# Attention with a feed-forward stage on one core: the products with v of the first eight heads in pieces, their sums in two banks of their own

## The chip, the core and the metric

One Trainium2 chip; the program runs on one of its cores. A core has TensorE (PE, matrix products; PEld is its weight load), VectorE (DVE), ScalarE (ACT), GpSimd (POOL) and SyncE (SP, which here only starts transfers). Each engine takes its instructions in the order in which they were written for it. Matrix products write to PSUM, which has eight banks of 512 fp32 values per partition; VectorE and ScalarE read them from there. The metric is the device time of one execution in microseconds. Time before: 1236.84 us, the median of 3 runs (1234.63 to 1239.13).

## The reference

For 8 batches and 8 heads with 576 positions and 64 values per head, attention with a block-causal mask (blocks of 64), then a feed-forward stage over all 4608 tokens:

```python
scores = scale * np.matmul(q, k.transpose(0, 1, 3, 2))
scores = np.where(mask, scores, -1000000000.0)
scores = scores - np.max(scores, axis=-1, keepdims=True)
attn = np.exp(scores)
attn = attn / (np.sum(attn, axis=-1, keepdims=True) + 1e-09)
out = np.matmul(attn, v)                # x: 4608 tokens x 512
h = x @ w_in                            # 512 -> 2048
sp = np.maximum(h, 0.0) + np.log1p(np.exp(-np.abs(h)))
g = h * erf(sp)
y = g @ w_out                           # 2048 -> 512
```

## The kernel before, in words

**Steps.** A loop `for n in range(N + 3)` (L684) runs over the 64 heads, software-pipelined. Step n holds: the load of head n+3 (L396 to L402: k and q into a ring of four tiles, by POOL's queue, and into a staging tile by SyncE's); the low parts of k and q on POOL (L405, L408), the latter for the first twelve heads behind two copies on ScalarE (L415); the scores of head n+2 for the row maxima (`maxes`: products L432, VectorE's reduction L435, five parts); the transposed maxima of head n+1 (L462, L464, a small transfer L465 into the ring); and the scores of head n once more, transposed, with the maxima taken off, and their exponentials (`probs`: products L478 and L479, ScalarE L483, six parts). In every even step from 2 on, `pv` (L502) takes the products of the probabilities of heads n-2 and n-1 with v. Four heads form a group `qd` of one load of v; NQ = 2 groups make a batch. In the step after a group's second pair, `normalise` (L579) transposes and inverts the row sums, scales the result and stores it to `x_d`, split into two fp16 parts.

**The rest of a step.** In the first twenty steps the weights are converted too (`conv`: load L115 on SyncE's queue, ScalarE L122 and L128, VectorE L123 to L125; then `split_w`, L148 and L149). The feed-forward stage (`moe1`: products L193 and L202, the function of `gate` between them) takes its turns in each step once the first batch has been stored, from step 10 on, and runs alone after the last head.

**Order.** Each part of a step is a list of small functions with a stretch of the step, from 0 to 1. `merged` (L210) gives entry i of a list of m the place lo + (hi - lo)(i + 0.5)/m and calls all of them by place. That order is the priority by which the framework's planner orders each engine's instructions; it works with modelled durations, and an instruction that is ready may be put before an earlier one that is not. Waits between engines are inserted by the framework.

**pv.** `go` (L518) handles one half of the 576 query positions (0 to 255, 256 to 575): for every key block of 128 up to the half's end it issues the products of both heads, 64 columns of the array each, summing into one bank `u`; after the last key block ScalarE copies the sum out (L530). The first half has two key blocks, the second five. `sums` (L544) adds the probabilities up with products of 32 columns of ones (L550) into one bank, which ScalarE reads (L552, L553). For the first three batches the operands are fp32, and each product is two passes of TensorE. `pv` returns two entries: all of `go` for both halves, and `sums`.

**Banks.** PSUM is split into three pools: `ps_a` (four banks), `ps_h` (two, the hidden values of the feed-forward stage) and `ps_o` (two, its outputs). `bank` (L321) hands out a bank for everything in attention. Until the first feed-forward job is loaded it goes round in eights: two requests of eight get a bank of `ps_h`, one of `ps_o`, five of `ps_a`. After that all come from `ps_a`. A request waits until the last reader of the bank's previous content is through.

Of the kernel before, what the change touches and what calls it, by code (L numbers as in the profile page):

```python
# [9 lines left out]
F32 = mybir.dt.float32  # L10
# [22 lines left out]
def tile_attention_moe(ctx: ExitStack, tc: tile.TileContext, qk, v, w, maskrows, selws, out):  # L33
# [5 lines left out]
    P = 128  # L39
    NCC = DM // P  # L40
    SCALE = 0.125
    NQ = H // 4
# [16 lines left out]
    ps_o = ctx.enter_context(tc.tile_pool(name="ps_o", bufs=2, space=PSUM))  # L59
# [70 lines left out]
    def scale_w(g, bank):  # L130

        rs = cpool.tile([P, 2], F32, name=f"wrs{g}")
        nc.vector.tensor_reduce(out=rs, in_=wss[g], axis=AX.X, op=ALU.add)
        pt = bank(f"wt{g}")
        nc.tensor.matmul(pt[:, :2], lhsT=ones, rhs=rs, start=True, stop=True)
        e = cpool.tile([P, 2], F32, name=f"we{g}")
        nc.vector.tensor_copy(e, pt[:, :2])
        nc.vector.tensor_scalar(out=i32(e), in0=i32(e), scalar1=23, scalar2=None, op0=ALU.logical_shift_right)
        nc.vector.tensor_scalar(out=i32(e), in0=i32(e), scalar1=131, scalar2=None, op0=ALU.add)
        nc.vector.tensor_scalar(out=i32(e), in0=i32(e), scalar1=1, scalar2=None, op0=ALU.logical_shift_right)  # L140
        powers(wsb[g][:, 0:2], wsb[g][:, 2:4], e, 15)
# [156 lines left out]
    with tc.tile_pool(name="apool", bufs=2) as apool, tc.tile_pool(name="spool", bufs=1) as spool, \  # L298
# [22 lines left out]
        def bank(name):  # L321

            turn.append(0)
            k = len(turn) % 8 if not loaded else 0
            if k in (2, 5):
                return ps_h.tile([P, 512], F32, tag="h", name=name)
            if k in (3,):
                return ps_o.tile([P, 512], F32, tag="o", name=name)
            return ps_a.tile([P, 512], F32, tag="a", name=name)

        def load_v(b, qd, src):
# [12 lines left out]
        def scale_v(b, qd, v32, vt):  # L344

            nm = f"{b}_{qd}"
            vm = apool.tile([P, 1], F32, tag="vm", name=f"vm{nm}")
            nc.vector.tensor_reduce(out=vm, in_=v32, axis=AX.XY, op=ALU.max, apply_absolute_value=True)
            pt = bank(f"vt{nm}")
            nc.tensor.transpose(out=pt[:1, :P], in_=vm, identity=ident)  # L350
            if qd == 0:
                nc.vector.tensor_reduce(out=top_v[b], in_=pt[:1, :P], axis=AX.X, op=ALU.max)
                if b < B32:
                    return
            vs = apool.tile([1, 2], F32, tag="vs", name=f"vs{nm}")
            vs_[b, qd] = vs
            e = apool.tile([1, 2], F32, tag="ve", name=f"ve{nm}")
            if qd:
                nc.vector.tensor_reduce(out=e[:, :1], in_=pt[:1, :P], axis=AX.X, op=ALU.max)
                nc.vector.tensor_tensor(out=e[:, :1], in0=e[:, :1], in1=top_v[b], op=ALU.max)  # L360
            nc.vector.tensor_scalar(out=i32(e[:, :1]), in0=i32(e[:, :1] if qd else top_v[b]), scalar1=23, scalar2=None, op0=ALU.logical_shift_right)
            nc.vector.tensor_scalar(out=i32(e[:, :1]), in0=i32(e[:, :1]), scalar1=77, scalar2=197, op0=ALU.max, op1=ALU.min)
            powers(vs[:, 0:1], vs[:, 1:2], e[:, :1], 10)
# [138 lines left out]
        def pv(qd, pp, prs, V, usb, rs):  # L502

            vv = V[1:]
            terms = ((0, 0), (1, 0), (0, 1)) if len(vv) > 1 else ((0, 0),)
            one, tail = (ones32, ones32t) if len(vv) > 1 else (ones[:, :32],) * 2
            st = {}

            def ranges(q0, q1):

                for j in range(5):
                    if starts[j] < q1:
                        a = max(q0, starts[j])
                        pt, c = offs[j]
                        c += a - starts[j]
                        yield j, min(P, S - j * P) if len(vv) == 1 else P, a - q0, pt, slice(c, c + q1 - a)

            def go(hf, j0, j1):  # L518
                q0, q1 = halves[hf]
                todo = list(ranges(q0, q1))  # L520
                if j0 == 0:
                    st[hf] = bank(f"u{qd}_{pp}_{hf}")
                u = st[hf]
                for j, kk, a, pt, cs in todo[j0:j1]:
                    for iv, ip in terms:
                        for hd in range(2):
                            nc.tensor.matmul(u[64 * hd : 64 * hd + 64, a : q1 - q0], lhsT=vv[iv][:kk, 2 * pp + hd, j, :], rhs=prs[hd][pt][ip][:kk, cs],  # L527
                                             start=j == 0 and (iv, ip) == terms[0], stop=j == todo[-1][0] and (iv, ip) == terms[-1])
                if j1 >= len(todo):
                    nc.scalar.copy(usb[:, q0:q1], u[:, : q1 - q0])  # L530


            order = []
            for hf, (q0, q1) in enumerate(((0, SH), (SH, S))):
                at, todo = 0, list(ranges(q0, q1))
                for n_, (j, kk, a, pt, cs) in enumerate(todo):
                    for k in range(len(vv)):
                        first, last = n_ == 0 and k == 0, n_ == len(todo) - 1 and k == len(vv) - 1
                        for hd in range(2):
                            order.append((at, hf, hd, k, j, kk, a, q1 - q0, pt, cs, first, last))  # L540
                        at += q1 - q0 - a
            order.sort(key=lambda o: o[0])

            def sums(n0, n1):  # L544
                if n0 == 0:
                    st["us"] = bank(f"us{qd}_{pp}")
                u = st["us"]
                for _, hf, hd, k, j, kk, a, w_, pt, cs, first, last in order[n0:n1]:
                    g = 2 * hf + hd
                    nc.tensor.matmul(u[32 * g : 32 * g + 32, a:w_], lhsT=(one if j < 4 else tail)[:kk, :], rhs=prs[hd][pt][k][:kk, cs], start=first, stop=last)  # L550
                if n1 >= len(order):
                    nc.scalar.activation(rs[:, : S - SH], u[:, : S - SH], AF.Identity, bias=eps)  # L552
                    nc.scalar.activation(rs[:64, S - SH :], u[:64, S - SH : SH], AF.Identity, bias=eps[:64])  # L553

            return [lambda: (go(0, 0, 2), go(1, 0, 5)), lambda: sums(0, len(order))]

        known = []
# [126 lines left out]
        for n in range(N + 3):  # L684
# [14 lines left out]
            qd = n // 4 + 1  # L699
# [8 lines left out]
            if n % 2 == 0 and 2 <= n <= N:  # L708
                j = n // 2 - 1
                qd, pp = divmod(j, 2)  # L710
                usbs[j] = apool.tile([P, S], F32, tag="usb", name=f"usb{j}", bufs=2)
                steps = pv(qd, pp, [prs.pop(2 * j), prs.pop(2 * j + 1)], vs[qd], usbs[j], rss[j % 2])
                lists.append((late("pv", steps), 0, 1))
                if pp == 1:
                    normals[n + 1] = qd
            if n in normals:
                qd = normals.pop(n)
# [67 lines left out]
```

## Time and profile before

| | |
|---|---|
| median of 3 runs | 1236.84 us (1234.63 to 1239.13) |
| the profiled execution | 1233.12 us, span 1231.3 us |
| mean granted clock of TensorE | 0.968 |
| TensorE busy | 1149.8 us (93%) |
| ScalarE busy | 863.3 us (70%) |
| VectorE busy | 824.7 us (67%) |
| POOL busy | 478.7 us (39%) |
| products with v, L527, in the first 180 us | 176 recorded passes |

The page gives shares over the whole span, which here mixes three stages: the first 100 us or so, where attention alone runs beside the conversion of the weights; the long middle, where attention and the feed-forward stage share the engines; and the end, where the feed-forward stage runs alone. In a row of a timeline stand the start, the duration, the engine, the line, what is written from what, the shapes and the count of merged instructions; in brackets the idle time before it and what ended it. A row of waits reads: who waited for whom, us in total, times, the longest. The granted clock is a share of full speed.

### The profile page before, as it was taken

Reading aid. Unit: us, or ns where it says so; the run is one execution under the profiler, and the core shown is the slowest. Engines: PE = TensorE matmul, PEld = TensorE weight load, DVE = VectorE, ACT = ScalarE, POOL = GpSimd, SP = SyncE. Lnnn points to the kernel's source line nnn. Section 1 sums busy time; section 2 is a strip of 40 time slices with the busy share of each in tenths; the row PEclk is TensorE's granted clock in tenths of the full one; section 3 lists DMA queues with packets and bytes.
Section 4 is the critical chain, followed back from the end, with each engine's and each line's share of the span. In section 5 each row is a group of like instructions: output and inputs, shape, how many; then the busy total and the mean of one; then the engine's idle time right before and its main releaser. Section 6 shows DMA issues by size and latency. Waiting matters only on the chain.

```text
span 1231.3 us, 23115 instructions
## 1 busy us (share of the span) xinstructions
PE 1149.8 (93%) x8874; PEld 796.0 (65%) x8874; DVE 824.7 (67%) x1559; ACT 863.3 (70%) x1675; POOL 478.7 (39%) x459
## 2 busy tenths in 40 slices
PE   6867899899999999999999999999989999999997
PEld 3545666566666667767666676776766766666663
DVE  5877887797577767677667666666667644455555
ACT  4665777577677776777777676777767776766664
POOL 7454545535444544445354444435444322100000
PEclk9876899989999999999999999999999999999999
DMA  8676667735545455453554455444544221221202
GB/s 231 171 211 161 166 186 219 179 91 122 120 133 138 110 129 124 129 136 102 124 137 95 114 125 121 115 124 116 120 114 108 57 67 57 72 69 52 65 23 85
DMA packets 94091, 148.19 MB, mean 120 GB/s; under 512 B 7610, under 2 KB 44794, under 8 KB 93982
## 3 DMA queue, kind: packets, MB, share of 16 engines
q1 hardware_dynamic: 69696, 93.34, 24.9%
q0 software_dynamic: 23616, 53.15, 20.3%
q8 instruction: 70, 1.15, 0.4%
q10 hardware_dynamic: 670, 0.23, 0.1%
q14 instruction: 39, 0.32, 0.1%
HBM read 118.15 MB, written 28.31 MB: 119 GB/s over the span
## 4 chain that ended last, share of the span: by engine, by line
PE 34%; DVE 26%; ACT 25%; DMA 7%; issue 6%; POOL 2%; ACTq 0%; DVEq 0%; SPq 0%; POOLq 0%
PE m_h L193 11%; PE o L202 10%; DVE m_r L165 6%; DVE m_r L166 5%; DVE m_r L167 5%; PE u L527 4%; ACT m_r L162 4%; ACT m_r L161 4%; ACT m_r L164 4%; ACT m_r L163 4%; ACT m_gh L168 3%; DVE mx L435 3%; PE s L432 2%; PE t L478 2%; DMA qk<-qk 2%
## 5 line engine op out<-in xcount | busy, mean ns | idle before, releaser
L193 PE MATMUL m_h<-xh,w 128*128 128x256 f16 x2304 | 473.7, 275 | 13.1 <-DVE m_r L167 12.1
L193 PEld LDWEIGHTS <-w 128*128 128x128 f16 x3456 | 327.3, 99 | 147.0 <-issue 18.1
L202 PE MATMUL o<-w,m_gh 128*128 128x512 f16 x1152 | 332.9, 382 | 4.7 <-ACT m_gh L168 3.8
L193 PE MATMUL m_h<-xl,w 128*128 128x256 f16 x1152 | 316.3, 275 | 0.0
L169 POOL TENSOR_TENSOR m_gl<-m_r,m_gh 128x512 f16<-128x512 f32 x114 | 136.1, 1193 | 267.7 <-ACT m_gh L168 234.7
L435 DVE TENSOR_REDUCE mx<-s 64x1 f32<-64x288 f32 (+4 forms) x384 | 173.9, 469 | 93.5 <-PE s L432 92.9
L165 DVE SCALAR_TENSOR_TENSOR m_r<-m_r,m_r 128x512 f32<-128x512 f32 x144 | 116.2, 807 | 166.4 <-ACT m_r L164 161.6
L168 ACT CAST m_gh<-m_r 128x512 f16<-128x512 f32 x144 | 88.9, 617 | 173.3 <-DVE m_r L167 171.5
L202 PE MATMUL o<-w,m_gl 128*128 128x512 f16 x576 | 203.7, 384 | 0.0
L483 ACT ACTIVATE p<-t 128x288 f32<-128x288 f32 (+4 forms) x384 | 143.8, 383 | 68.4 <-PE t L479 60.4
L478 PE MATMUL t<-qk 69*128 69x288 f32 (+4 forms) x384 | 167.8, 438 | 13.1 <-DVE mx L435 6.1
L432 PE MATMUL s<-qk 68*64 68x288 f32 (+3 forms) x384 | 148.5, 421 | 24.6 <-DMA qk<-qk 18.6
L408 POOL TENSOR_TENSOR qk<-st,qk 64x576 fp32r<-64x576 f32 x64 | 94.9, 1484 | 128.8 <-DMA qk<-qk 121.0
L161 ACT ACTIVATE m_r<-m_h,c,bs 128x512 f32<-128x512 f32 (+3 forms) x192 | 123.9, 665 | 28.9 <-PE m_h L193 27.4
L202 PEld LDWEIGHTS <-m_gh 128*128 128x128 f16 x1152 | 100.4, 98 | 60.9 <-issue 6.9
L495 DVE TENSOR_TENSOR p<-p,p 128x832 f16<-128x832 f32 x80 | 81.6, 1020 | 62.6 <-ACT p L494 62.5
L479 PE MATMUL t<-qk 128*128 128x288 f32 (+4 forms) x384 | 120.7, 316 | 0.0
L166 DVE SCALAR_TENSOR_TENSOR m_r<-m_r 128x512 f32<-128x512 f32 x144 | 116.7, 810 | 3.2
L405 POOL TENSOR_TENSOR qk<-st,qk 64x576 fp32r<-64x576 f32 x64 | 98.5, 1539 | 29.6 <-ACT qk L415 13.0
L163 ACT ACTIVATE m_r<-m_r,c 128x512 f32<-128x512 f32 x144 | 103.7, 720 | 2.7 <-ACT m_r L162 0.6
L164 ACT ACTIVATE m_r<-m_r,c 128x512 f32<-128x512 f32 x144 | 103.6, 719 | 2.2 <-ACT m_r L163 0.3
L162 ACT ACTIVATE m_r<-m_r,c 128x512 f32<-128x512 f32 x144 | 103.7, 720 | 2.0
(113 smaller groups left out, 1459.9 us busy)
## 6 DMA issues: line engine op xcount, KB each, us to landing
qk<-qk POOLq DMA_DIRECT2D x52, 432.0 KB, 4.7
st<-qk SPq DMA_DIRECT2D x64, 288.0 KB
qk<-qk POOLq DMA_DIRECT2D x64, 288.0 KB, 5.0
raw<-w SPq DMA_DIRECT2D x32, 512.0 KB
v<-v SPq DMA_DIRECT2D x16, 640.0 KB
x_d<-xs POOLq DMA_DIRECT2D x32, 288.0 KB, 3.3
xh<-x_d SPq DMA_DIRECT2D x36, 256.0 KB
xl<-x_d SPq DMA_DIRECT2D x36, 256.0 KB
```

Of the source, the lines that this page charges most:

```text
L161: nc.scalar.activation(r0s[:, :, lo:hi], h[:, :, lo:hi], AF.Tanh, bias=const(p1), scale=bss[b][g][:, 0:1])
L162: nc.scalar.activation(r1, r0, AF.Square, bias=const(b1), scale=a1)
L163: nc.scalar.activation(r0, r1, AF.Square, bias=const(b2), scale=a2)
L164: nc.scalar.activation(r0, r0, AF.Square, bias=const(b3), scale=a3)
L165: nc.vector.scalar_tensor_tensor(out=r0, in0=r0, scalar=c4, in1=r1, op0=ALU.add, op1=ALU.mult)
L166: nc.vector.scalar_tensor_tensor(out=r0, in0=r0, scalar=c5, in1=r0, op0=ALU.add, op1=ALU.mult)
L193: nc.tensor.matmul(h[:, k, :], lhsT=wf[:, a, sl], rhs=x[:, cc, :], start=cc == 0 and i == 0, stop=cc == NCC - 1 and i == 2)
L202: nc.tensor.matmul(o[c], lhsT=a[:, sl], rhs=wf[:, b_, :], start=u == u0 and k == 0 and not lo and b_ == 2, stop=u == u1 - 1 and k == nu - ...
L432: nc.tensor.matmul(dst[:r, :w_], lhsT=qh[:K, i * P : i * P + r], rhs=kh[:K, k0 : k0 + w_], start=True, stop=True)
L435: nc.vector.tensor_reduce(out=mx[:r, col : col + 1], in_=src, axis=AX.X, op=ALU.max, negate=True)
L478: nc.tensor.matmul(s[:kk, :w_], lhsT=kh[:K, ks], rhs=qh[:K, q0 : q0 + w_], start=True, stop=False)
L483: nc.scalar.activation(p32s[part][:kk, c : c + w_ - skip], s[:kk, skip:w_], AF.Exp, scale=SCALE)
```

## The change

In the groups of the first batch (qd below NQ, heads 0 to 7, emitted in steps 2, 4, 6 and 8) `pv` returns eight entries instead of two: one per key block, two for the first half and five for the second, and `sums`. The banks of these sums come from `ps_o`, one per half, outside the rotation. `bank` no longer hands out `ps_o`; the one request in eight that got it now gets `ps_a`. Later groups are as before.

```diff
             if k in (2, 5):
                 return ps_h.tile([P, 512], F32, tag="h", name=name)
-            if k in (3,):
-                return ps_o.tile([P, 512], F32, tag="o", name=name)
             return ps_a.tile([P, 512], F32, tag="a", name=name)
...
                 if j0 == 0:
-                    st[hf] = bank(f"u{qd}_{pp}_{hf}")
+                    nm = f"u{qd}_{pp}_{hf}"
+                    st[hf] = bank(nm) if qd >= NQ else ps_o.tile([P, 512], F32, tag="o", name=nm)
                 u = st[hf]
...
+            if qd < NQ:
+                return [lambda hf=hf, j=j: go(hf, j, j + 1) for hf, k in ((0, 2), (1, 5)) for j in range(k)] + [lambda: sums(0, len(order))]
             return [lambda: (go(0, 0, 2), go(1, 0, 5)), lambda: sums(0, len(order))]
```

## The prediction

> **What bounds the kernel now.** I read the page first, then the stretches of the span that hold the changed steps, then the waits of that part, and last the engines in order of time. "Step n" is one turn of the loop over heads; the changed groups are emitted in steps 2, 4, 6 and 8. In order of time the first scores of those steps start at 33.1, 48.4, 67.0 and 92.7 us, which cuts the windows below (columns: length; busy time of PE, PEld, DVE, ACT, POOL; granted clock; DMA share; GB/s).
>
> ```profile
> span 1231.3 us, 23115 instructions
> PEclk9876899989999999999999999999999999999999
> ```
>
> ```profile
> 33.10:48.40 15.30, 14.48 (x99) 9.54 (x99) 11.92 (x35) 10.38 (x27) 6.16 (x6) 0.80 0.52 142
> 48.40:67.00 18.60, 13.69 (x101) 9.00 (x102) 17.02 (x41) 11.81 (x33) 8.70 (x9) 0.90 0.79 240
> 67.00:92.70 25.70, 20.10 (x122) 14.21 (x123) 17.77 (x39) 17.72 (x44) 16.20 (x16) 0.70 0.65 183
> 92.70:106.30 13.60, 11.04 (x81) 7.33 (x81) 9.66 (x23) 8.36 (x23) 4.49 (x4) 0.75 0.67 214
> ...
> 200.00:1231.00 1031.00, 990.42 (x7849) 690.58 (x7848) 669.35 (x1220) 735.82 (x1374) 374.80 (x341) 0.99 0.41 107
> ```
>
> After 200 us TensorE is busy 990.42 of 1031.00 us: that part is a fixed list of products, untouched by the change, and a lead won earlier arrives at the end almost whole. From 33 to 106 us no engine is full for long (PE 59.31 of 73.20 us, the sum of the four rows), the clock is below 1, and the time goes to chains that run through several engines.
>
> ```profile
> ACT usb L530 <- PE u L527: 5.6, 4, 2.1
> ...
> PE s L432 <- ACT usb L530: 0.9, 1, 0.9
> ...
> PE t L478 <- DVE mx L435: 0.3, 1, 0.3
> ```
>
> These are the waits of 30 to 106 us that the change addresses: ScalarE stands 5.6 us, at four places, until the block of L527 ends, and once TensorE waits for a bank that holds such a sum. In order of time on TensorE:
>
> ```profile
> 34.79 5.25 PE L527 MATMUL u<-p,v 128*64 128x256 f32 x28
> ...
> 41.97 1.74 PE L550 MATMUL us<-p,ones 128*32 128x384 f32 x32
> 43.64 0.42 PE L478 MATMUL t<-qk 69*128 69x320 f32 x1
> ...
> 48.41 0.39 PE L432 MATMUL s<-qk 68*128 68x256 f32 x1 [0.67 <-DMA qk<-qk]
> ...
> 50.54 4.21 PE L527 MATMUL u<-p,v 128*64 128x256 f32 x28
> ...
> 56.87 0.35 PE L432 MATMUL s<-qk 68*64 68x288 f32 x1 [0.93 <-ACT usb L530]
> ...
> 57.56 1.74 PE L550 MATMUL us<-p,ones 128*32 128x384 f32 x32
> ...
> 59.57 0.31 PE L479 MATMUL t<-qk 128*128 128x320 f32 x1
> ...
> 67.02 0.55 PE L432 MATMUL s<-qk 68*128 68x256 f32 x1 [3.53 <-DMA qk<-qk]
> ...
> 72.38 0.44 PE L478 MATMUL t<-qk 69*128 69x288 f32 x1
> 72.62 0.44 PE L479 MATMUL t<-qk 128*128 128x288 f32 x1
> 72.99 4.92 PE L527 MATMUL u<-p,v 128*64 128x256 f32 x28
> ...
> 79.44 0.51 PE L479 MATMUL t<-qk 128*128 128x448 f32 x2
> 79.88 1.74 PE L550 MATMUL us<-p,ones 128*32 128x384 f32 x32
> ...
> 93.71 4.16 PE L527 MATMUL u<-p,v 128*64 128x320 f32 x20
> ```
>
> All 28 passes (14 products, two passes each) run in one go, 4.2 to 5.3 us; the row sums of L550, 1.74 us, stand ahead of the head's last scores (43.64 and 59.57 us), and only those free the ring slot for a later head's load. How that shows on the other engines:
>
> ```profile
> 38.77 1.32 DVE L124 SCALAR_TENSOR_TENSOR w<-a,w 128x512 int32<-128x512 int32 x1 [1.74 <-ACT a L122]
> ```
>
> ```profile
> 60.30 0.62 POOL L396 DMA_DIRECT2D qk<-qk  x1 [0.82 <-PE t L478]
> ...
> 78.64 0.74 POOL L615 DMA_DIRECT2D x_d<-xs  x1
> 79.47 1.82 POOL L405 TENSOR_TENSOR qk<-st,qk 64x576 fp32r<-64x576 f32 x1
> ...
> 100.20 1.56 POOL L405 TENSOR_TENSOR qk<-st,qk 64x576 fp32r<-64x576 f32 x1 [2.30 <-ACT qk L415]
> ```
>
> ```profile
> 36.41 0.37 ACT L530 COPY usb<-u 128x256 f32<-128x256 f32 x1 [1.10 <-PE u L527]
> ...
> 77.96 0.42 ACT L530 COPY usb<-u 128x320 f32<-128x320 f32 x1 [2.15 <-PE u L527]
> ...
> 97.91 0.43 ACT L530 COPY usb<-u 128x320 f32<-128x320 f32 x1 [1.59 <-PE u L527]
> ```
>
> **The change, part by part.** The products, copies and DMAs stay the same in number and size. What changes is their place, their banks, and the array's alternation.
>
> *Order.* A step's list is spread evenly over the step. With two entries the block sits at 0.25 and the row sums at 0.75; with eight, the seven pieces sit at 0.06, 0.19, 0.31, 0.44, 0.56, 0.69 and 0.81, the row sums at 0.94. The six parts of the scores to be exponentiated sit at 0.08 to 0.92. So each piece falls between scores that feed VectorE and ScalarE, the copy of the second half moves from 0.25 to 0.81, and the row sums pass behind the head's last scores. I price this step by step:
>
> - Step 2. ScalarE waits 1.10 us for the block, and VectorE then 1.74 us for the conversion queued behind it. Upper bound: both, 2.84 us; lower: 0, as the first half's copy still stands early. I take 1.5, nearest to VectorE's own wait, since VectorE is what runs full next (17.02 of 18.60 us from 48.4).
> - Step 4. The 0.93 us wait for the bank goes. The row sums (1.74 us busy) no longer stand ahead of the last scores, so the load issued at 60.30 goes out as much earlier, and the 3.53 us wait at 67.02 shrinks by it; the sums then run inside that wait. Together 2.67, lower bound 0 (if VectorE, full here, holds the scores instead). I take 2.6.
> - Step 6. ScalarE's 2.15 us wait goes, but what it holds back, L405 on POOL, could begin hardly earlier: POOL issues the store of L615 at 78.64 for 0.74 us, to 79.38, and L405 starts at 79.47. Bounds 0.09 and 2.15; I take 0.8, nearer to POOL's row. The row sums here already follow the last scores (79.44, then 79.88): nothing.
> - Step 8. ScalarE waits 1.59 us; behind it POOL stands idle 2.30 us for L405, and SyncE's next loads stand behind that in its queue. I take 1.6 for it. The row sums' 1.74 us free the next ring load too, but the loads then share the DMA; half, 0.8. Bounds 0 and 3.33.
>
> Sum: 1.5 + 2.6 + 0.8 + 2.4 = 7.3 us. In each case what is late next is a load of a head or of weights: the rows show that the chain goes on there.
>
> ```profile
> 60.30 6.59 DMA qk<-qk
> ...
> 102.22 9.04 DMA raw<-w
> ```
>
> *Array alternation.* Before, TensorE leaves full-width products twice per changed step; after, eight times. Entering the block costs: scores of 288 columns start 0.24 us apart (72.38, 72.62), but the block starts 0.37 after the last of them (72.99), so 0.13 more. No row isolates leaving it; bounds 0 and another 0.13. Six more entries are 0.78 us per step, with the exits 1.56. I charge entries alone, nearest to the one row there is, in steps 2, 4 and 8, where TensorE lies on the chain; step 6 hangs on POOL. That is 2.3 us, with bounds 0 and 6.2 (four steps with exits).
>
> The Trainium skill, "TensorEngine Tiling (Array Packing)", section Key Properties, speaks against this change: changing the tiling mode drains the TensorE, and the pieces are 64 columns wide while the scores are full width. The 0.13 us row agrees with it in kind; by the rule every exit drains as well, and the sum would be the one with exits paid, 7.3 − 3 × 1.56 = 2.6 us of gain; that is the lower end of the forecast's range below and lies in its 0.09 of no change.
>
> *Banks.* The sums leave the general rotation for the two banks of the feed-forward outputs, which are otherwise empty until the first job is loaded, after step 8. In return one in eight of the other requests moves from those two banks to the four general ones. Four banks then serve six of eight requests rather than five, but the two requests per step that held a bank longest are gone. I count this as nothing beyond the 0.93: from 33 to 106 us the scores at L478 wait for VectorE's bank reads once, 0.3 us, and more such waits would first fall into the odd steps, which end in DMA waits of 0.67 and 3.53 us. Without that cover they would cost about 0.3 each.
>
> *Moved work and queues.* The row sums' two ScalarE readings come after the last exponentials, and in steps 5 and 9 the transposes of the normalisation may wait for them; the odd step's scores stand between, and I add nothing. One wait is new in kind: the next head's first exponential writes the probability buffer that the row sums read last. But TensorE runs the sums ahead of that head's scores, so the wait is over when the scores arrive; were it not, everything in ScalarE's queue would stand behind it, up to the sums' 1.74 us in each of four steps. The loads of v, in the odd steps, still come after the last piece. No DMA is moved past another by the edit itself.
>
> Net: 7.3 − 2.3 = 5.0 us. The profiled execution took 1233.12 us (span 1231.3 and 1.8 around it), so 1228.1 by its own time; it lies 3.7 us below the median shown, 1236.84. Against the median: 1231.8 us.
>
> **The rivals.**
>
> *The clock stays half (slower).* The gate opens late in the block, which is dense work:
>
> ```profile
> 38.00:39.00 1.00, 1.00 (x6) 0.44 (x4) 0.23 (x1) 0.97 (x3) 0.87 (x1) 0.50 0.00 0
> 39.00:40.00 1.00, 1.00 (x12) 0.40 (x9) 1.00 (x1) 0.30 (x1) 0.93 (x2) 0.89 0.36 86
> ...
> 112.00:113.00 1.00, 0.87 (x4) 0.44 (x2) 1.00 (x2) 0.32 (x2) 0.99 (x1) 0.50 0.00 0
> ```
>
> In step 2 it opens in the sixth microsecond after the start at 33.14; at 112 us, with gaps, it stands at 0.50. If pieces between waiting scores leave such gaps, the work that now runs at full clock from about 40 us to the last scores at 43.64 + 0.42, some 4.1 us, takes 8.2. One step of that kind takes 4.1 of the 5.0; from two on it decides: 8.2 − 5.0 = 3.2 us slower, with three 7.3; about 1241. For it: the clock is 0.70 to 0.90 in all four windows. Against it: a half clock makes TensorE the slowest engine, so its queue is seldom empty, and the pieces fill time between scores. The Trainium skill, "TensorE: Matmul & The Clock Gate", section A second HAM failure mode, describes this: small idle stretches between groups of products, as banks are cycled, let the gate close again and again. The row at 112 us agrees; the dense steps at hand do not show it yet.
>
> *Hidden anyway (no change).* Loads leave earlier but land no earlier, because DMA (share 0.52 to 0.79 on average, and 6.59 and 9.04 us for transfers on the chain) and POOL set the pace. For it: step 6 as above. Against it: the share leaves room, and the 3.53 us wait began with the issue at 60.30. Only the bank wait remains, less switching: 1236.
>
> *All bounds reached.* 2.84 + 2.67 + 2.15 + 3.33 = 11.0, less 2.3: 8.7 us, 1228.
>
> *It does not do what it says.* The order is only a priority, and the program's planner may pull pieces together again (in step 8 only 20 of the 28 passes are left in the block). Then only the bank moves: about 1236.5.
>
> **How the numbers follow.** Forecast (2.5 to 7.5 us gained) 0.45; all bounds 0.13; hidden 0.16; not as said 0.04; half clock 0.22. About 0.3%, 3.7 us, is what a measurement of this kernel can tell from no change. Of the forecast's share 0.36 lies beyond that and 0.09 within. Faster: 0.36 + 0.13 + 0.01 = 0.50; same: 0.09 + 0.16 + 0.02 = 0.27; slower: 0.22 + 0.01 = 0.23. The likeliest case's own range is 1229 to 1234. For 8 in 10 it reaches to the full 11.0 us without switching cost (1226) and to two to three cold steps or no gain with nearly all exits paid (1242).
>
> **What would show it.** Right: L527 spread over each even step in groups of four passes; the waits of ScalarE's L530 for L527 down from 5.6 us to under 2; no wait of L432 for L530; L550 behind the last L478/L479 of its head; the 3.53 us DMA wait about 1.7 us shorter; the scores that start now at 106.3 us about 5 us earlier, and the same distance at the end. Wrong: granted clock in 33 to 106 us lower than the four rows above (half clock); new waits of TensorE for VectorE's L435 of over 3 us in sum (banks); the same load landing at the same time (hidden); L527 with far longer busy time at equal clock (switching).

## The result, and the profile after

The changed kernel took 1242.17 us (median of 20, 1233.42 to 1253.83), the kernel before 1233.90 us (median of 20 beside it, 1226.88 to 1241.37). The ratio is 1.0059, 95% interval 1.0041 to 1.0078: slower by 0.6%, which is 7.3 us by the ratio; the medians lie 8.3 us apart. The forecast was 1231.8 us and a gain. The profiled execution of the changed kernel is the fastest of its 20, so a second profile of the same kernel, 1241.22 us long, is read beside it where a loss at the end is meant.

In the code after, the lines named here stand one or two lower: `u` is L526 (was L527), `us` L549 (L550), `usb` L529 (L530), the scores L430, L476 and L477 (L432, L478, L479), the row maxima L433 (L435), the ring loads L394 to L400 (L396 to L402), ScalarE's copies for POOL L413 (L415).

The page of the changed kernel, span and chain of work that ended last:

```profile
span 1231.6 us, 23115 instructions
...
PE 36%; ACT 26%; DVE 26%; issue 5%; DMA 5%; POOL 1%; ACTq 0%; DVEq 0%; SPq 0%; POOLq 0%
```

The same stretches of the changed kernel as in the prediction (length; busy time of PE, PEld, DVE, ACT, POOL; granted clock; DMA share; GB/s):

```profile
33.10:48.40 15.30, 14.53 (x99) 8.50 (x98) 11.74 (x34) 9.32 (x25) 8.76 (x8) 1.00 0.62 168
48.40:67.00 18.60, 16.20 (x100) 8.84 (x102) 15.37 (x36) 13.78 (x37) 9.93 (x9) 0.90 0.75 229
67.00:92.70 25.70, 24.14 (x106) 12.59 (x103) 16.44 (x39) 13.84 (x35) 10.44 (x11) 0.60 0.52 161
92.70:106.30 13.60, 10.47 (x85) 6.27 (x83) 11.86 (x24) 9.95 (x26) 8.32 (x8) 1.00 0.75 212
...
200.00:1231.00 1031.00, 991.09 (x7866) 691.14 (x7864) 671.16 (x1223) 737.87 (x1379) 375.70 (x342) 0.99 0.41 108
```

TensorE was busy 20.10 of 25.70 us between 67.0 and 92.7 us before; now it is busy 24.14 us with fewer instructions (106 recorded against 122). Over the four rows its busy time went from 59.31 to 65.34 us. The clock is no lower on the whole: 1.00, 0.90, 0.60 and 1.00 against 0.80, 0.90, 0.70 and 0.75 (the second profile of the changed kernel has 0.80, 0.99, 0.61 and 1.00). The last row is as before, so what changed lies ahead of 200 us.

The busy time of the two kinds of product whose order the change touches, from 14 to 116 us; in each fence the first row is `u`, the second `us`. Before:

```profile
14.00:116.00 102.00, 20.08 (x112) 10.34 (x112) 3.20 (x8) 0.77 0.71 197
14.00:116.00 102.00, 6.96 (x128) 4.62 (x128) 2.88 (x8) 0.77 0.71 197
```

The changed kernel:

```profile
14.00:116.00 102.00, 25.72 (x112) 9.23 (x112) 3.13 (x8) 0.78 0.69 195
14.00:116.00 102.00, 11.31 (x128) 5.02 (x128) 3.05 (x8) 0.78 0.69 195
```

The second profile of the changed kernel:

```profile
14.00:116.00 102.00, 27.10 (x112) 9.57 (x112) 3.14 (x8) 0.76 0.70 196
14.00:116.00 102.00, 10.62 (x128) 4.96 (x128) 3.06 (x8) 0.76 0.70 196
```

The same 112 and 128 passes at the same granted clock of the stretch (0.77; 0.78 and 0.76) take 27.04 us before and 37.03 and 37.72 us after: 10.0 and 10.7 us more of recorded time. Weighted by the time of these passes alone, the granted clock is even higher after, 0.80 and 0.79 against 0.73, so the clock doesn't explain it. How it comes about shows in step 6 of the changed kernel, in order of time on TensorE:

```profile
74.69 0.44 PE L477 MATMUL t<-qk 128*128 128x288 f32 x1
75.06 1.34 PE L526 MATMUL u<-p,v 128*64 128x320 f32 x4
76.33 0.58 PE L476 MATMUL t<-qk 69*128 69x256 f32 x1
76.71 0.42 PE L477 MATMUL t<-qk 128*128 128x256 f32 x1
76.92 0.44 PE L476 MATMUL t<-qk 69*128 69x288 f32 x1
...
77.40 0.95 PE L430 MATMUL s<-qk 68*128 68x256 f32 x3
...
81.64 1.49 PE L549 MATMUL us<-p,ones 128*32 128x384 f32 x2
...
84.67 1.50 PE L549 MATMUL us<-p,ones 128*32 128x384 f32 x12
...
86.53 1.00 PE L549 MATMUL us<-p,ones 128*32 128x256 f32 x2
...
87.96 1.08 PE L549 MATMUL us<-p,ones 128*32 128x192 f32 x16
```

Entering the piece costs as foreseen: it starts 0.37 us after a product of 288 columns that otherwise takes 0.24. But the product behind it, 256 columns, takes 0.38 us (76.33 to 76.71), where the same size takes 0.21 one row on: leaving costs 0.17. And the row sums, which were one run of 32 passes in 1.74 us, are torn into four by the planner, at 1.49, 1.50, 1.00 and 1.08 us, 5.07 us in all; the 1.74 us were at full clock, the first three of the four runs at half, so part of this difference is the clock. Counted over TensorE's timeline up to 118 us, the products with v and those of the row sums (below: narrow products, 64 or 32 columns of the array) form 10 unbroken runs before and 31 after, in both profiles. Divided by the 21 added runs, the 10.0 and 10.7 us are about 0.5 us each; that is a quotient and not yet a price.

The scores of the last 64 positions, which also take 64 columns, aren't in this count, and they show no such cost: two of them with 256 columns of data, and the product behind them, start 0.20 and 0.11 us apart (92.24, 92.44, 92.55 us in the changed kernel), two that take 128 columns of the array 0.19 and 0.12 (91.67, 91.86, 91.98). So a small number of columns isn't dear by itself. The products with v and of the row sums differ from the scores in two more ways: neighbours use different columns of the array side by side, and each is two passes where a score is one.

The chain of waits of the changed kernel in the same step (start, us, what):

```profile
72.83 0.64 PE t L476
...
73.74 0.62 PE u L526 x2
...
81.71 1.42 PE us L549 x2
...
90.62 0.25 PE s L430 x2
```

From 72.8 to 90.9 us every piece of the chain is TensorE. The scores that waited 3.53 us for their load before and started at 67.02 wait for no DMA any more, and yet they start at 77.40 (the row above), with no idle time of TensorE before them: its queue comes to them only then. The waits from 30 to 106 us that belong to it:

```profile
POOL qk L394 <- PE t L477: 12.2, 2, 6.6
...
ACT usb L529 <- PE u L526: 0.7, 2, 0.4
...
PE s L430 <- DVE mx L433: 0.6, 1, 0.6
```

ScalarE's wait for the block did go, from 5.6 to 0.7 us (1.3 in the second profile). In its place POOL waits 12.2 us (10.5) for the last scores of a head before it can issue a ring load. Before, that was

```profile
POOL qk L396 <- PE t L479: 3.0, 2, 2.2
```

and 0.8 us for L478. Those issues, before (the row of 60.30 us stands in the prediction):

```profile
72.29 0.62 POOL L396 DMA_DIRECT2D qk<-qk  x1 [0.80 <-PE t L479]
...
81.23 0.61 POOL L396 DMA_DIRECT2D qk<-qk  x1
...
275.92 0.65 POOL L400 DMA_DIRECT2D qk<-qk  x1
```

and in the second profile of the changed kernel:

```profile
60.59 0.62 POOL L394 DMA_DIRECT2D qk<-qk  x1
...
75.56 0.62 POOL L394 DMA_DIRECT2D qk<-qk  x1 [4.19 <-PE t L477]
...
88.85 0.60 POOL L394 DMA_DIRECT2D qk<-qk  x1 [5.79 <-PE t L477]
...
281.00 0.65 POOL L398 DMA_DIRECT2D qk<-qk  x1
```

The load that went out at 60.30 us before goes out at 60.59; the next at 75.56 instead of 72.29, the one after at 88.85 instead of 81.23, 7.6 us late. At 276 us the load is 5.1 us late. In the fastest execution the first of these loads went out early, at 58.22, and the third still 7 us late:

```profile
58.22 0.73 POOL L394 DMA_DIRECT2D qk<-qk  x1
...
88.18 0.60 POOL L394 DMA_DIRECT2D qk<-qk  x1 [6.64 <-PE t L477]
```

The lag of step 6 doesn't travel to the end as it is. The load issued at 102.15 us before goes out at 103.09 in the fastest execution and at 103.79 in the second, only 0.9 and 1.6 us late; a lag of 6.7 and 7.6 us stands again at 144 us (143.94 against 150.66 and 151.53), and at 276 us it is 0.9 and 5.1. The fastest execution took 1233.42 us, as long as the profiled one of before, 1233.12. The scores that started at 106.27 us start at 110.10 and 110.81, 3.8 and 4.5 us later, where the prediction had them 5 us earlier:

```profile
110.10 0.63 PE L430 MATMUL s<-qk 68*128 68x256 f32 x2
```

By what path the added TensorE time of steps 2 to 8 becomes the 7.3 us at the end is therefore not shown step by step.

### The profile page after: what moved, and what is told of

The parts are those of the page before. It is cut to its first block, busy times and chain, and to the rows that moved or that the text cites. A ratio compares the mean times of both kernels' runs of the same rounds, so it can differ in the third digit from the quotient of the medians.

```text
span 1231.6 us, 23115 instructions
## 1 busy us (share of the span) xinstructions
PE 1159.3 (94%) x8874; PEld 795.2 (65%) x8874; DVE 824.9 (67%) x1559; ACT 863.7 (70%) x1675; POOL 477.9 (39%) x459
## 4 chain that ended last, share of the span: by engine, by line
PE 36%; ACT 26%; DVE 26%; issue 5%; DMA 5%; POOL 1%; ACTq 0%; DVEq 0%; SPq 0%; POOLq 0%
PE m_h L193 11%; PE o L202 10%; DVE m_r L165 6%; DVE m_r L166 6%; DVE m_r L167 5%; ACT m_r L162 5%; ACT m_r L161 5%; ACT m_r L164 4%; ACT m_r L163 4%; PE u L526 4%; ACT m_gh L168 3%; PE t L476 3%; PE s L430 2%; DVE mx L433 2%; PE t L477 2%
## 5 line engine op out<-in xcount | busy, mean ns | idle before, releaser
L193 PE MATMUL m_h<-xh,w 128*128 128x256 f16 x2304 | 472.8, 275 | 11.0 <-DVE m_r L167 10.6
L433 DVE TENSOR_REDUCE mx<-s 64x1 f32<-64x288 f32 (+4 forms) x384 | 173.3, 469 | 94.7 <-PE s L430 86.9
L476 PE MATMUL t<-qk 69*128 69x288 f32 (+4 forms) x384 | 169.1, 441 | 11.3 <-DVE mx L433 5.6
L430 PE MATMUL s<-qk 68*64 68x288 f32 (+3 forms) x384 | 149.7, 422 | 13.3 <-DMA qk<-qk 6.4
L477 PE MATMUL t<-qk 128*128 128x288 f32 (+4 forms) x384 | 121.9, 318 | 0.0
L166 DVE SCALAR_TENSOR_TENSOR m_r<-m_r 128x512 f32<-128x512 f32 x144 | 113.5, 788 | 3.2
```

The source lines that it names most:

```text
L166: nc.vector.scalar_tensor_tensor(out=r0, in0=r0, scalar=c5, in1=r0, op0=ALU.add, op1=ALU.mult)
L193: nc.tensor.matmul(h[:, k, :], lhsT=wf[:, a, sl], rhs=x[:, cc, :], start=cc == 0 and i == 0, stop=cc == NCC - 1 and i == 2)
L430: nc.tensor.matmul(dst[:r, :w_], lhsT=qh[:K, i * P : i * P + r], rhs=kh[:K, k0 : k0 + w_], start=True, stop=True)
L433: nc.vector.tensor_reduce(out=mx[:r, col : col + 1], in_=src, axis=AX.X, op=ALU.max, negate=True)
L476: nc.tensor.matmul(s[:kk, :w_], lhsT=kh[:K, ks], rhs=qh[:K, q0 : q0 + w_], start=True, stop=False)
L477: nc.tensor.matmul(s[:kk, :w_], lhsT=klh[:, ks], rhs=qhl[:, q0 : q0 + w_], start=False, stop=True)
```

## The experiments

Four explanations stood against each other. **Width**: each change between full-width and narrow products stops TensorE's overlap on the way in and on the way out, and the change adds such alternations. **Clock**: without the dense block the gate stays half open. **Banks and warm-ups**: taking the third request out of the rotation delays scores, or lets the planner place the first products of the kernel badly. **Ring slots**: freeing a slot of the ring earlier or later is worth what the prediction gave it. All ratios below are to the kernel before, run beside it on the same chip.

**The changed kernel once more, and its two halves.** The changed kernel unaltered:

> The changed kernel once more, unaltered, for a second profile and a second ratio. Two theories of the loss. Clock: the pieces of the products with v, scattered between scores, leave TensorE at half clock in more of steps 2 to 8. Warm-up: the twenty warm-up products, which shared the output banks with one request in eight, now all run at 8 to 15 us, and TensorE is cold from about 19 to 33 us. Both expect a ratio of 1.004 to 1.008 here, as measured first; the first profile was the fastest of its 20 runs, so a second one should have a span some 5 to 10 us longer, and show where. A ratio below 1.002 would say that the loss was chance.

Measured 1.0054 (1.0029 to 1.0078). The loss repeats. Next, only the rotation loses its third request; the products stay in two entries and in rotating banks:

```diff
-            if k in (3,):
-                return ps_o.tile([P, 512], F32, tag="o", name=name)
```

> The kernel before, with one edit alone: the request in eight that got an output bank gets a general one. The products with v stay one block and in the rotation. In the program's order the twenty warm-up products move ahead exactly as in the changed kernel. Warm-up theory: ratio 1.004 to 1.008, TensorE at half clock from 19 to 33 us. Clock theory: within 0.3% of before (0.997 to 1.003), as the block is intact.

Measured 0.9982 (0.9954 to 1.0009): no loss. It has 10 narrow runs up to 118 us, as before, one of them already of step 10. The eight entries alone, with the banks of before:

```diff
+            if qd < NQ:
+                return [lambda hf=hf, j=j: go(hf, j, j + 1) for hf, k in ((0, 2), (1, 5)) for j in range(k)] + [lambda: sums(0, len(order))]
```

> The kernel before, with the eight entries alone: the banks are handed out as before, the third request included. The warm-up products stand where they stood before; the products with v are in pieces. Clock theory: ratio 1.004 to 1.008, granted clock in 33 to 106 us below before's. Warm-up theory: not slower, 0.993 to 1.002, since my terms for the order then remain.

Measured 1.0074 (1.0042 to 1.0105), with 33 narrow runs. The busy time of `u` and of `us` in this kernel:

```profile
14.00:116.00 102.00, 27.78 (x112) 9.18 (x112) 3.12 (x8) 0.76 0.70 197
14.00:116.00 102.00, 8.81 (x128) 5.32 (x128) 3.06 (x8) 0.76 0.70 197
```

36.59 us, 9.6 more than before: the order alone is enough for the whole loss. In this kernel the clock is lower too, 0.71 from 33 to 106 us against 0.78 before, as the clock explanation had it, so the two aren't told apart here. The other half, both edits of the banks without the eight entries:

```diff
-            if k in (3,):
-                return ps_o.tile([P, 512], F32, tag="o", name=name)
...
-                    st[hf] = bank(f"u{qd}_{pp}_{hf}")
+                    nm = f"u{qd}_{pp}_{hf}"
+                    st[hf] = bank(nm) if qd >= NQ else ps_o.tile([P, 512], F32, tag="o", name=nm)
```

> The changed kernel without the eight entries: banks as changed, products with v emitted as one block and row sums as before. In the program's order the planner nevertheless takes the block apart (groups of 1, 1, 4 and 8 products in step 2, two of them a step early), and the warm-up products move ahead. Warm-up theory: 1.004 to 1.008, the same as the third request alone. Clock theory: 1.002 to 1.006, since the pieces are there, in fewer groups. If it equals the changed kernel, the eight entries themselves cost nothing.

Measured 1.009 (1.0054 to 1.0125). That looks like a cost of banks, but the timeline shows otherwise: with a bank free at any time, the planner takes the block apart by itself.

```profile
23.93 1.12 PE L526 MATMUL u<-p,v 128*64 128x256 f32 x2
25.41 1.33 PE L526 MATMUL u<-p,v 128*64 128x320 f32 x2
```

These are products of step 2, run in step 1. The changed kernel does the same: its first pieces of step 2 run at 23.7 us. In this kernel there are 22 narrow runs, 12 more than before; `u` is busy 27.23 us and `us` 7.79, together 8.0 more than before. Twelve runs at 0.5 us are 6 us, the measured loss is some 11: for this kernel the count explains about half, and the rest is open.

**Clock.** Two kernels built on the changed one. Each puts added products, full width, ahead of a changed step's first product with v, in the bank that this product then overwrites: one of 64 columns of data, or six of 256. The added products also keep the pieces from running a step early, so the first of the two kernels tests whether that is the loss.

```diff
                 u = st[hf]
+                if qd < NQ and hf == 0 and j0 == 0:
+                    for _ in range(1):      # the other kernel: range(6), 256 columns
+                        nc.tensor.matmul(u[:, :64], lhsT=ones, rhs=prs[1][1][0][:, 704:768], start=True, stop=True)
```

> The changed kernel, with one small product of 64 columns added ahead of the first piece of each changed step, into the same bank and overwritten by it. It reads the newest probabilities of the second head, so no piece can be put before its own step; the pieces then stand as the prediction had them, in groups of 2 to 9 among the scores, row sums behind the last scores. Theory A (pieces scattered among scores do not open the clock gate): ratio 1.003 to 1.008, granted clock 33 to 106 us at or below the 0.78 that before has there. Theory B (the loss comes from pieces that the planner pulls into earlier steps, ahead of the scores that free the next load): 0.993 to 1.001.

> As the run with the small product, but six full-width fp32 products of 256 columns each stand there instead of the one, 2.6 us per changed step at full clock and 5.2 at half, 10 to 21 us of TensorE work over four steps. Theory A: they open the gate as the block did, so the granted clock from 33 to 106 us is 0.05 or more above that of the run with the small product, and the time is within +0.3% of that run in spite of the added work (at most 4 us more). Theory B: the clock does not matter; the added work lies on the chain, 8 us or more over the run with the small product.

Measured 1.0038 (1.0009 to 1.0066) with one product and 1.0048 (1.0021 to 1.0075) with six. With no piece ahead of its step most of the loss stays, so the early pieces aren't the main cause. All engines from 33 to 106 us, with one added product:

```profile
33.00:106.00 73.00, 62.76 (x345) 34.85 (x345) 49.63 (x120) 43.38 (x112) 30.54 (x31) 0.73 0.63 179
```

with six:

```profile
33.00:106.00 73.00, 64.39 (x394) 43.48 (x396) 54.36 (x124) 46.57 (x117) 34.82 (x32) 0.83 0.66 184
```

With the heavy products the granted clock is 0.83 instead of 0.73. Of the 49 instructions more in this stretch (394 against 345) 40 are the added passes themselves, and the whole takes the same. That is what the clock explanation expected: 10 to 21 us of added work, by the estimate above, were carried for 0.1% of time, well within the intervals, so in this pair the clock is worth about what the added products cost. It doesn't show that the clock is without effect, nor that a higher clock alone would take the loss away.

**How much is torn.** Three kernels without the third request, with the row sums and the block moved in larger parts. First, three entries, one for each half and one for the row sums:

```diff
+            if qd < NQ:
+                return [lambda: go(0, 0, 2), lambda: go(1, 0, 5), lambda: sums(0, len(order))]
```

> The kernel before without the third request (which alone measured 0.998), and the products with v as three entries: first half at 0.17, second half at 0.5, row sums at 0.83. In the program's order ten products of a step stay nearly together and the other four go singly or in threes. Theory A: between before and the changed kernel, 0.999 to 1.004, since ten products (some 3.0 to 3.7 us) are about what the gate needed. Theory B: 0.996 to 1.000, as nothing leaves its step.

Measured 1.0043 (1.0018 to 1.0069), with 19 narrow runs; `u` is busy 25.00 us, `us`, in one run each time, 6.96 as before. Then the block whole and at its old place, the row sums alone late, behind the head's last scores:

```diff
+            if qd < NQ:
+                nop = lambda: None
+                return [nop, nop, lambda: (go(0, 0, 2), go(1, 0, 5))] + [nop] * 6 + [lambda: sums(0, len(order))]
```

> The kernel before without the third request, the block whole at 0.25, only the row sums moved from 0.75 to 0.95, behind the head's last scores. This tests my term for the row sums alone: 1.7 us in step 4 and some of it in step 8, so 2 to 3 us below the run without the third request: ratio 0.994 to 0.998. If the term was wrong, 0.998 to 1.002. Theories A and B both expect no loss.

Measured 1.0018 (0.9995 to 1.0041), with 10 narrow runs. No gain from late row sums is to be seen. Last, block and row sums both late:

```diff
+            if qd < NQ:
+                nop = lambda: None
+                return [nop] * 8 + [lambda: (go(0, 0, 2), go(1, 0, 5)), lambda: sums(0, len(order))]
```

> The kernel before without the third request, with the whole block moved from 0.25 to 0.85 of its step and the row sums from 0.75 to 0.95, so that nearly all of the 6 us of 64- and 32-column work stands behind most of the head's scores. If the release of the ring slot by the last scores sets the pace, as my terms for steps 4 and 8 assumed, the loads go out up to 5 us earlier per changed step and the time falls by 4 to 10 us (0.992 to 0.997). If the work only changes places on a chain that runs through TensorE anyway, 0.998 to 1.004.

Measured 1.0030 (1.0003 to 1.0057): the scores that free the ring slot run ahead of the whole block, and nothing is won by it. It has 12 narrow runs.

Across these kernels the recorded time of `u` and `us` together goes with the loss better than the count of runs does. Over the 27.04 us of before it is 0.9 us longer with the row sums late, 2.7 with all late and 4.9 in halves, at 1.0018, 1.0030 and 1.0043; it is 8.0 longer with the banks alone, 9.6 with the split alone and 10.0 in the changed kernel, at 1.0090, 1.0074 and 1.0059. Within the second three the order is reversed, and the kernel with one added product stands apart: 9.6 us more, 18 added runs and only 1.0038. Each of these times comes from one profile.

**The width by itself.** Two kernels whose instructions stand in the same order. The block stays whole; between its key blocks stand five added products per changed step, all of 64 columns of data and into a bank that nothing reads. In one they are 64 columns of the array wide, as the block itself, in the other 128:

```diff
                 for j, kk, a, pt, cs in todo[j0:j1]:
+                    if qd < NQ and j:
+                        nc.tensor.matmul(ps_w[:64, :64], lhsT=ones[:, :64], rhs=prs[1][1][0][:, 704:768], start=True, stop=True)
                     # the other kernel: ps_w[:128, :64], lhsT=ones[:, :128]
```

> The control: the same five added products per changed step, but 64 columns wide, as the products with v are, so no change of width within the block. Theory C: 0.2 to 0.6 us per block over the run without the third request for the added work itself, time within 0.3% of it. Theory D: the same as with the wide ones.

> The kernel before without the third request, the block whole and in its place; between its key blocks stand five small added products per changed step (64 columns of fp32, full width of 128 columns of ones, into the unused output bank). The program's order is the same as in the run with the narrow ones. Theory C (each change between 64-column and full-width products drains TensorE, on the way in and out): the time from the block's first product to the next score is 5 times 0.2 to 0.3 us longer at full clock (1.0 to 1.5 us, twice that at half clock) than with narrow ones, and the whole time 2 to 6 us above it. Theory D (only the scatter in time matters, not the alternation): no difference over 0.3 us per block.

Measured 1.0030 (1.0001 to 1.0060) at half width and 1.0116 (1.0076 to 1.0156) at full width. The difference is 0.86% of 1234.7 us, 10.6 us, for 20 excursions to full width and back; the two intervals taken together give about 0.4 to 1.4%. In order of time on TensorE, full width, once at full clock and once at half:

```profile
56.82 0.76 PE L527 MATMUL u<-p,v 128*64 128x320 f32 x4
57.51 0.43 PE L524 MATMUL warm<-p,ones 128*128 128x64 f32 x2
57.87 0.76 PE L527 MATMUL u<-p,v 128*64 128x320 f32 x4
...
81.34 1.34 PE L527 MATMUL u<-p,v 128*64 128x320 f32 x4
82.61 0.69 PE L524 MATMUL warm<-p,ones 128*128 128x64 f32 x2
83.23 1.34 PE L527 MATMUL u<-p,v 128*64 128x320 f32 x4
```

and half width, where the same two passes slip in between the products:

```profile
55.41 0.22 PE L524 MATMUL warm<-p,ones 128*64 128x64 f32 x1
...
56.06 0.22 PE L524 MATMUL warm<-p,ones 128*64 128x64 f32 x1
...
80.83 0.31 PE L524 MATMUL warm<-p,ones 128*64 128x64 f32 x1
...
82.11 0.31 PE L524 MATMUL warm<-p,ones 128*64 128x64 f32 x1
```

One round of four passes of 320 columns and two of 64 takes 1.05 us (56.82 to 57.87) at full width and 0.65 (55.41 to 56.06) at half width, at full clock; 1.89 (81.34 to 83.23) and 1.28 (80.83 to 82.11) at half clock. Out and back therefore costs 0.40 us at full clock and 0.61 at half. Twenty of them are 8 to 12 us, and 10.6 arrived at the end; expected were 0.2 to 0.3 us at full clock and 2 to 6 us in all. The granted clock from 33 to 106 us was 0.80 with narrow products and 0.73 with wide ones, so part of the 10.6 us may come by way of the clock. The rows of the weight loads show one thing that is lost: at half width the weights of an added product are loaded from 55.14 us, 0.27 us ahead of the product and while the product before still runs; at full width load and product start together, at 56.45. The wide products also load twice as many columns, 0.19 against 0.14 us a load, and this pair doesn't separate that from the change of width. All its products are two passes; what the change from one-pass scores to two-pass products adds in the changed kernel wasn't tested. The Trainium skill, "TensorEngine Tiling (Array Packing)", section Key Properties, says that changing the tiling mode drains the TensorE; these rows agree, and they give the price that the page doesn't.

The kernel without the third request was run once more beside these:

> The kernel before without the third request, once more, beside the three runs that build on it. 0.996 to 1.000 if its first 0.998 holds; a second profile of an intact block for the comparison of TensorE's time in L526 and L548 (some 27 to 28 us for both in steps 2 to 8, against 37 in the changed kernel).

Measured 0.9997 (0.9975 to 1.0019). With 0.9982 before, the edit of the rotation by itself costs nothing and brings nothing that can be told. No kernel here is shown to beat the one before.

## Why the prediction was wrong

It forecast a net gain of 5.0 us, from gains of 7.3 and an alternation of 2.3. The loss of about 7.3 us comes from the second term, and most of the first is not seen to arrive.

**Array alternation: this step failed.** The prediction charged 0.13 us for each of 18 entries, 2.3 us, and set the upper bound at 6.2. Measured are 10.0 and 10.7 us of recorded TensorE time for 21 added runs, about 0.5 each, and 0.40 to 0.61 for an excursion in the pair above. The prediction's own sign of this came: the products with v take far longer, 25.72 us against 20.08, at equal clock. Three things were mis-sized. The exit costs as much as the entry or more (0.17 beside 0.13 in step 6), which the prediction held for possible and left out, though the Trainium skill's rule, which the prediction cites, named it. The overlap of a product with its neighbours and their weight loads is lost at each change: the round trip costs 0.61 us at half clock, twice the 0.30 that the two edges show. And the row sums, priced as one run of 1.74 us, were torn as well (5.07 us in step 6, most of it at half clock), because the planner puts a ready instruction ahead of others; the prediction asked whether the planner would pull pieces together, and it pulled them further apart, the first pieces of step 6 to 54.6 us, into step 4.

**TensorE off the path in step 6: this step failed too.** The prediction let the alternation count in steps 2, 4 and 8 only, since step 6 hung on POOL. In the changed kernel TensorE carries every piece of the chain there from 72.8 to 90.9 us, and in this step a ring load falls 7 us behind. Of that lag 0.9 and 1.6 us are left at the next step's load, so how much of the final loss comes from step 6 stays open.

**The order, term by term.** The foreseen signs came: ScalarE's wait for the block fell from 5.6 us to 0.7, no scores wait for `usb` any longer, and in the fastest execution the load of 60.30 us went out 2.1 us earlier, near the 2.67 of step 4. But in the other profile the same load went out at 60.59, and a lead at 58 us is a lag of 7 by 88 us. The late row sums (1.74 of step 4, 0.8 of step 8) were also tried alone: 1.0018, with an interval up from 0.9995, so at most some 0.6 us of gain. Freeing the ring slot still earlier, with the block late, gave 1.0030. A wait of 1 to 2 us for the block was work that TensorE had to do at some time; the rows of step 6 show it waited for elsewhere, by POOL for 12.2 us. If all of the 10 us of added TensorE time reached the end, some 3 of the 7.3 us of gain arrived; that split isn't measured.

**The half clock.** This rival came nearest in number, 1241 against 1242.17, but for another reason than it gave. It placed the loss in step 2, where the clock is now 1.00 in one profile and 0.80, as before, in the other, and in gaps between waiting pieces. Between 33 and 106 us the changed kernel has the higher clock, 0.84 in this row and 0.82 in the second profile, where the same row of before has 0.78:

```profile
33.00:106.00 73.00, 65.45 (x384) 36.23 (x383) 55.21 (x129) 46.89 (x120) 37.45 (x36) 0.84 0.64 188
```

It fell in step 6 alone, from 0.70 to 0.60 and 0.61, and there TensorE had hardly a gap. Each excursion is dearer at half clock (0.61 against 0.40 us), and two kernels in pieces do have a lower clock, 0.71 with the split alone and 0.73 with one added product; how their loss divides between width and clock isn't settled.

**Banks.** Costed at nothing beyond the 0.93 us; 0.9982 and 0.9997 agree. TensorE's waits for VectorE's reads of L433 grew from 0.3 to 1.0 us for products, and with those of weight loads from 1.0 to 3.1, which is at the mark that the prediction had set; but without the third request weight loads alone wait 4.9 us for L433, and that kernel isn't slower. What the prediction didn't see is that with private banks the planner also has no bank to wait for that would hold the block together: the banks alone have 22 narrow runs.

**The whole.** The measured median lies 10.4 us above the forecast and 0.2 us past the upper end of the range, 1242. At the measured 0.5 us its own 18 entries would have been 9 us against 7.3 of gain, and the sign would have been the other.

## What to carry to other kernels

Before a block of narrow products is cut into pieces between full-width ones, price each piece with a whole excursion, in and out, at the clock granted in that stage: 0.4 us at full clock here, 0.6 at half, both for two-pass products of 64 columns, and ask whether the pieces' neighbours can still overlap. A wait behind a dense block need not be a gain in store when the same engine must do the work anyway; look at which engine has the chain once the wait is gone. And a private buffer is a change of order too: where a planner may run what is ready, the wait for a buffer can be what keeps a block whole.

## What the runs showed of the hardware

**Busy but not open.** Before, in step 6, the block began at 72.99 us and the clock rose between 76 and 77, 3 to 4 us later; in step 2 it rose between 39 and 40, 4 to 5 us after the block's start at 34.79. In step 6 of the changed kernel it took longer. One-microsecond rows:

```profile
73.00:74.00 1.00, 1.00 (x4) 0.63 (x4) 1.00 (x3) 1.00 (x3) 0.00 (x0) 0.50 0.79 324
...
87.00:88.00 1.00, 1.00 (x8) 0.34 (x8) 1.00 (x4) 0.94 (x4) 0.00 (x0) 0.83 0.00 0
```

From 73 to 87 us TensorE is recorded full in every microsecond, and the clock stays at 0.50 until 87. Ends of products are modelled in these records, so what is recorded as busy here may partly be the draining between widths; that reading fits the rows and isn't proved by them. Torn pieces don't always keep the clock down: in steps 2 and 4 of the same execution it was 1.00 and 0.90. In the trace of before, the stretches of one clock up to 142 us are 3.4, 6.8, 10.2, 13.6, 17.1 and 20.5 us long, multiples of 3.4 us, so the moment of a rise says little to the microsecond.

**Two passes, as dear as twelve.** At 81.64 us a run of only two passes of the row sums takes 1.49 us, at 84.67 one of twelve 1.50. Thirty-two passes in one run take 1.74 us at full clock. The single records show part of the reason. The two passes at 81.64 are one product, which writes to 32 columns of the array; the second starts 0.64 us behind the first, with no other product of the row sums beside them. In the run of twelve, products on other columns run at the same time, and in the run of 32 before, the first four passes start within 0.02 us. What else fills a short run was not isolated.
